# Two common steps, 32 row forms from a table, and loads moved behind a group's first results: attention with routed experts on one core

## The chip, the cores and the metric

The kernel runs on one core of one Trainium2 chip. The time is the device time of one execution in microseconds (us). Engines: PE is TensorE's matmul, PEld its weight load, DVE is VectorE, ACT is ScalarE, POOL is GpSimd, SP is the engine that issues most DMAs.

## What is computed

An attention with a window of local keys and a few global ones (batch 4, 8 heads, 768 positions, 64 per head) gives 3072 rows of 512. Each row goes to one of eight experts:

```python
logits = x @ w_gate
expert_idx = np.argmax(logits, axis=1)
...
gate_w = probs[np.arange(N), expert_idx]
for e in range(E):
    mask = expert_idx == e
    ...
    h = np.maximum(xe @ w1[e], 0.0)
    ye = h @ w2[e]
    out[mask] = gate_w[mask, None] * ye
```

`w1` is 512 x 1024 and `w2` is 1024 x 512 for each expert, all in float32. How many rows an expert gets is known only at run time.

## The kernel before

The first part (to about 160 us) is attention in 24 blocks of 128 rows. Each row is written to a place in HBM that belongs to its expert, and the experts' row counts are made on DVE. The second part takes the experts as *groups* in the order 0, E, 1, 2, ... 7: group 0 is expert 0 without the last sequence's rows, E is the late rest of expert 0 (`plain`, at most 128 rows), and the others are whole experts. This text calls the groups by their expert.

**A group.** Its rows are split in two halves of up to 256 (even and odd rows). `up` (line 993) and `down` (line 1006) multiply with a scheme of seven products of quarter matrices in place of eight (`seven`, line 882). `up` calls it twice (the columns of `w1` in two halves, j = 0 and 1), `down` once: 21 steps. A step of `up` is 4 matmuls of 128 x 128 weights by n rows, a step of `down` 8, where n is the number of rows in a half. DVE and ACT take each product out of PSUM: `one` is copied to p1 by ACT (L904), `two` adds to u2 on DVE (L908), `three` gives c11 through ACT (L913), `four` gives u3 (L919), `five`, `six` and `last` give c22, c21 and c12 (L935, L940, L974). `two` and `four` use the same PSUM bank Y, so `four` can't start before u2 is formed. The operations of DVE and ACT always take all 256 columns, whatever n is.

**Forms.** PE alone has code for several n: `SIZES` (line 675) holds 17 of them, 128 to 256 by 8. `tables` (line 754) works out an index from the group's row count on DVE, with an add, a shift, two copies of types and bounds. `f.hint` reads the index into a register of PE at the group's start, and names the branch target ahead; `emit_forms` (line 271) writes one copy of the group's steps for each size, and a branch with a table of equal strides (L277) goes to the one wanted. Products inside such a copy are cut to n columns (line 259).

**Common steps.** The first steps of a group are not in the forms, so that the branch need not be known at once. With `common` the four steps `one` to `four` of j = 0 are written once for 208 columns (`COMMON`). Forms over 208 make up for the columns past 208 in `rest` (line 921), which is put with `five`. It holds five products, three operations of DVE and two of ACT; DVE and ACT run theirs in every form.

**Order of the work.** The order on each engine is the order in which the code records operations. `group` (line 1329) does this: `run` goes through the steps, and `at_(i, ...)` puts operations behind step i. In a group behind its `one` come two blocks of the previous group's results (`y_out`, j = 1 and 3: four transposes on PE, a gating on ACT, L860, and a scatter on POOL), then `two`, the blocks 0 and 2, `three` and `four`, and then the branch (lines 1360 to 1368). DVE also forms the sums of the weight quarters (`own`, L738 to L741): two behind `one`, one behind `two`.

**Loads.** All are issued by SP in order, and an issue that has to wait holds those behind it. A group's start issues `load_x` for the next group (eight DMAs of rows and two of gate values). Step 10 writes blank rows for the group after next on POOL. Step 14 (`D`) issues the first weights of the group after next, four DMAs of 512 KB, and step 20 (`D + 6`) the second weights, four more (lines 1420 to 1424). There is one buffer for rows and two for weights.

Of the kernel before, what the change touches and what calls it, by code (L numbers as in the profile page):

```python
# [24 lines left out]
class Flow:  # L25
# [214 lines left out]
    def emit(self, op, sems, n, more=0):  # L240
        self.wait(op, sems)
        args, kw = op["args"], op["kw"]
        if op["name"] == "await":
            return
        if op["name"] == "number":
            ap, label = args
            self.loads[label] = self.nc.values_load(
                ap, min_val=0, max_val=1, skip_runtime_bounds_check_because="a comparison's result")
            return
        if op["name"] == "load":  # L250
            index, n, label = args
            self.loads[label] = self.nc.tensor.value_load(index, min_val=0, max_val=n - 1)
            return
        if op["name"] == "hint":
            index, n, label = args
            self.hints[label] = self.loads[label], self.nc.tensor.switch_hint(self.loads[label], n, label)
            return
        if n is not None and op["dyn"]:
            n -= op["past"]
            args = tuple(a[:, 0:n] for a in args[:1]) + tuple(args[1:])  # L260
            kw = dict(kw, rhs=kw["rhs"][:, 0:n])
        call = getattr(self.engines[op["e"]], op["name"])
        where = dict(call=call, args=args, kw=kw)

        exec(_code(*op["at"]), where)
        if op["dma"]:
            where["inst"].then_inc(sems[op["proc"]], 16)
        elif op.get("told") or more:
            where["inst"].then_inc(sems[op["proc"]], int(bool(op.get("told"))) + more)
# [393 lines left out]
class Experts:  # L663
# [8 lines left out]


    P, E, CAP, LATE, COMMON = 128, 8, 512, 128, 208
    SIZES = list(range(128, 257, 8))

    def __init__(self, f, dims, psum, keep, wsets, work, zeros, ylast):
        self.f, self.psum, self.keep = f, psum, keep
# [65 lines left out]
    def slots_table(self):  # L744
        f, k, E = self.f, self.keep, self.E
        for j in range(4):
            f.pool.iota(k["slot4"][:, 0, j:j + 1], pattern=[[0, 1]], base=256 * (j // 2) + j % 2,
                        channel_multiplier=2, allow_small_or_imprecise_dtypes=True)
            f.pool.iota(k["slot4"][:, 1, j:j + 1], pattern=[[0, 1]], base=128 * j,
                        channel_multiplier=1, allow_small_or_imprecise_dtypes=True)  # L750
        f.pool.iota(k["gbase"][:], pattern=[[self.REGION, E + 1]], base=0, channel_multiplier=0,
                    allow_small_or_imprecise_dtypes=True)

    def tables(self, g0, g1, late=False):
        k, V = self.keep, self.f.dve
        n = g1 - g0
        shape = [self.P, n, 4]
        cnt = k["cnt"][:, g0:g1]
        sl = k["slot4"][:, int(late), :].unsqueeze(1).to_broadcast(shape)
        inv = k["inv"][:, g0:g1, :]  # L760
        V.tensor_tensor(inv, cnt.unsqueeze(2).to_broadcast(shape), sl, ALU.is_le)
        V.tensor_scalar(k["inv_i"][:, g0:g1, :], inv, float(2 ** 30), None, ALU.mult)
        V.tensor_scalar(k["is_i"][:, g0:g1, :], inv, 1.0, None, ALU.subtract)
        if late:
            return
        ki, kf = k["ki"][:, g0:g1], k["kf"][:, g0:g1]
        V.tensor_scalar(ki, cnt, 15.0, None, ALU.add)
        V.tensor_scalar(ki, ki, 4, None, ALU.logical_shift_right)
        V.tensor_copy(out=kf, in_=ki)
        V.tensor_scalar(kf, kf, 16.0, 0.0, ALU.subtract, ALU.max)  # L770
        V.tensor_scalar(k["index"][:, g0:g1], kf, 16.0, None, ALU.min)

    def blank(self, g):

# [107 lines left out]
    def seven(self, c, a, s, cols, order, dst, act, half=None, common=False, end=None):  # L882
# [9 lines left out]
        def bank(b):  # L892
            return self.psum[:, b, :].rearrange("p (t c) -> p t c", t=2)

        def mm(b, wq, xq, fresh, half=None, cut=slice(0, 256)):
            self.product(b, [c[wq][:, k, cols] for k in order], [xq[:, k, :] for k in order], fresh, half, cut)
# [18 lines left out]
                f.act.copy(dst["c11"], bank(X))  # L915

        def four():
            mm(Y, "t3", s[2], True, cut=some)
            V.tensor_tensor(u3[:, :, some], u2[:, :, some], bank(Y)[:, :, some], ALU.add)  # L919

        def rest():
            T = self.tbanks[self.tp ^ 1]
            mm(X2, "b11", a["a11"], True, cut=past)
            f.act.copy(p1[:, :, past], bank(X2)[:, :, past])
            mm(Y2, "t2", s[1], True, cut=past)
            V.tensor_tensor(u2[:, :, past], p1[:, :, past], bank(Y2)[:, :, past], ALU.add)
            mm(W2, "b11", a["a11"], True, cut=past)
            mm(W2, "b21", a["a12"], False, cut=past)
            f.act.activation(dst["c11"][:, :, past], bank(W2)[:, :, past], act)
            mm(T, "t3", s[2], True, cut=past)  # L930
            V.tensor_tensor(u3[:, :, past], u2[:, :, past], bank(T)[:, :, past], ALU.add)

        def five():
            mm(W, "t1", s[0], True)
            V.tensor_tensor(dst["c22"], u3, bank(W), ALU.add)  # L935
            relu(dst["c22"])
# [40 lines left out]
        if half:  # L977
            return [one, two, four_end, five_end, six, three, last_end]
        if common:
            return [one, two, three, four, lambda: [rest(), five()], six, last]  # L980
        return [one, two, three, four, five, six, last]

    def h_sums(self, j):
# [55 lines left out]
def kernel(  # L1039
# [46 lines left out]
        ("oh", [P, NBLK, E], BF16), ("slot_i", [P, 2, NBLK], I32), ("ok", [P, 8], F32),  # L1086
        ("flag", [P, 1], I32), ("far", [P, 1], F32), ("slot4", [P, 2, 4], F32), ("gbase", [P, E + 1], F32), ("cnt", [P, E + 1], F32),
        ("inv", [P, E + 1, 4], F32), ("is_i", [P, E + 1, 4], I32), ("padf", [P, E + 1, 4], F32), ("pad", [P, E + 1, 4], I32),
        ("inv_i", [P, E + 1, 4], I32), ("ki", [P, E + 1], I32), ("kf", [P, E + 1], F32),
        ("index", [P, E + 1], I32), ("gt", [P, E + 1, 4, 2], F32), ("to", [P, E + 1, 4], I32))}  # L1090
    ident, iota_p, col, before, ones, rev8, ebase, base_e, tokid = (
        keep[nm] for nm in ("ident", "iota_p", "col", "before", "ones", "rev8", "ebase", "base_e", "tokid"))
# [7 lines left out]
    with ExitStack() as stack:  # L1100
# [225 lines left out]
        for fn in ex.x_sums():  # L1326
            fn()

        def group(p):

            g = order[p]
# [4 lines left out]
            def at_(i, *fns):  # L1336
                todo.setdefault(i, []).extend(fns)
# [8 lines left out]
            if p:  # L1346

                prev = order[p - 1]
                if E not in (g, prev):
                    f.hint(*forms[g])  # L1350
                if nxt is not None and g != E:
                    ex.load_x(nxt, [f"pad{nxt}.{j}" for j in range(4)])
                if nxt is None:
                    f.number(keep["flag"][0:1, 0:1], "redo")
                outs = [0] if prev == E else [1, 3, 0, 2]
                own = ex.w_sums(g, True) + ex.w_sums(g, False) if ups else None
                if ups:
                    at_(0, own[3], own[4])
                    at_(1, own[5])
                    run(ups[:1], 0)  # L1360
                for j in outs[:2]:
                    ex.y_out(prev, j)
                if ups:
                    run(ups[1:2], 1)
                for j in outs[2:]:
                    ex.y_out(prev, j)
                if ups:
                    run(ups[2:4], 2)
            D = 14
            if g != E:  # L1370

# [31 lines left out]
            elif g == E:  # L1403
                sums, pieces, xs = ex.w_sums(1, True), ex.w_pieces(2), ex.x_sums()
                at_(0, sums[0], sums[1])
                at_(1, sums[2], check_sums)
                at_(2, check)
                at_(3, lambda: f.hint(*forms[1]), lambda: ex.x_in(1, 0), lambda: ex.x_in(1, 1), xs[0], xs[1])
                at_(4, xs[2], xs[3], lambda: ex.marks(1), *pieces[:4])
                at_(5, *pieces[4:])  # L1410
            else:
                if nxt is not None:
                    sums, xs = ex.w_sums(nxt, True), ex.x_sums()
                    at_(13, lambda: ex.x_in(nxt, 0))
                    at_(D + 1, lambda: ex.x_in(nxt, 1), sums[0])
                    at_(D + 3, xs[0], xs[1])
                    at_(D + 4, sums[1])
                    at_(D + 5, sums[2])
                    at_(D + 6, xs[2], xs[3], lambda: ex.marks(nxt))
                if after is not None:  # L1420
                    pieces = ex.w_pieces(after)
                    at_(10, lambda: ex.pads(after, ex.h[:, 2:4, 0]))
                    at_(D, *pieces[:4])
                    at_(D + 6, *pieces[4:])

            if g == E:
                ex.plain(0, lambda i: [fn() for fn in todo.pop(i, ())])
                return
            with f.forms(*forms[g]):
                run(ups[4:] if p else ups[2:], 4 if p else 2)  # L1430
                early = ((1, "act"), (3, "dve")) if nxt is None else ()
                run(ex.down(g, (lambda: [ex.y_out(g, j, on) for j, on in early]) if early else None), D)
            assert not todo, todo
# [440 lines left out]
```

## Time and profile before

| | us |
|---|---|
| runs | 500.08, 500.9, 501.0 (median 500.9) |
| profiled execution | 499.16, its span 497.3 |
| granted TensorE clock in it | 0.989 |
| PE busy | 474.0 (95% of the span) |
| DVE busy | 361.4 (73%) |
| all matmuls of the experts (L876) | 288.9 in 1760 rows of the trace |
| PE's last work ends at | 484.3 |

Each float32 matmul is two rows of the trace. Group 2 starts at 255.6 us, group 3 at 292.9, group 4 at 332.7, group 5 at 370.0, group 6 at 411.2 and group 7 at 451.0. The trace has the sequencer's instructions too (moves, branches, hints); the page doesn't count them as busy. A row of idle time names what ended it, as far as the profile can tell.

### The profile page before, as it was taken

How to read it: one execution, taken by the hardware profiler on the slowest of the kernel's cores; microseconds unless marked ns; L12 is line 12 of the kernel's file. 1: busy time of each engine (PE TensorE's matmuls, PEld its weight loads, DVE VectorE, ACT ScalarE, POOL GpSimd, SP SyncE). 2: the span in 40 equal slices, each digit the busy share in tenths (PEclk: the TensorE clock that was granted, in tenths of full speed). 3: DMA queues.
4: the chain of work that ended last, by engine and by line, in shares of the span. 5: the costliest groups of instructions: out<-in, count | busy, mean ns of one | idle time of the engine just before them, and what ended most of it. 6: DMA issues, size and time to landing. Idle time of an engine off the chain costs nothing. (4 is left out here: it accounts for less than half of the span.)

```text
span 497.3 us, 10822 instructions
## 1 busy us (share of the span) xinstructions
PE 474.0 (95%) x4413; PEld 448.9 (90%) x4413; DVE 361.4 (73%) x649; ACT 172.8 (35%) x309; POOL 167.1 (34%) x193
## 2 busy tenths in 40 slices
PE   7899999999998999999999999999999999999990
PEld 6788888887787899999999999999999999999980
DVE  6366779899886884766876886867877676777850
ACT  5665555653654230323123223214214204303410
POOL 2653578567775053302013213204304303003011
PEclk9999999999999999999999999999999999999995
DMA  9999999989524438896864764657567478001000
GB/s 174 204 244 244 198 240 259 235 202 242 149 88 86 171 129 189 207 258 148 189 207 120 186 213 112 155 177 179 128 202 177 111 186 237 3 1 55 14 26 30
DMA packets 120092, 79.24 MB, mean 159 GB/s; under 512 B 86170, under 2 KB 103066, under 8 KB 120020
## 3 DMA queue, kind: packets, MB, share of 16 engines
q1 hardware_dynamic: 112482, 63.52, 55.4%
q0 software_dynamic: 6480, 14.45, 8.1%
q8 instruction: 51, 0.84, 0.7%
q10 hardware_dynamic: 1058, 0.26, 0.3%
q14 instruction: 21, 0.17, 0.1%
HBM read 61.39 MB, written 23.71 MB: 171 GB/s over the span
## 5 line engine op out<-in xcount | busy, mean ns | idle before, releaser
L876 PE MATMUL psum<-arena 128*128 128x208 f32 (+5 forms) x1760 | 288.9, 325 | 0.2
L876 PEld LDWEIGHTS psum<-arena 128*128 128x128 f32 x1760 | 283.6, 190 | 1.8 <-ACT arena L904 0.6
L866 POOL DMA_INDIRECT out_dram<-arena,to x16 | 22.9, 1432 | 170.9 <-ACT arena L860 147.3
L529 DVE TENSOR_TENSOR arena<-psum,arena 128x1024 f32<-128x1024 f32 x40 | 48.3, 1218 | 28.1 <-PE psum L519 28.1
L537 ACT ACTIVATE arena<-arena 128x1024 f32<-128x1024 f32 (+1 forms) x48 | 47.4, 988 | 51.6 <-DVE arena L529 43.8
L543 POOL TENSOR_TENSOR arena<-arena 128x512 f32<-128x512 f32 x40 | 51.9, 1300 | 29.6 <-ACT arena L537 29.3
L900 ACT ACTIVATE arena<-arena 128x512 f32<-128x512 f32 x48 | 30.2, 630 | 53.6 <-DVE arena L935 33.4
L519 PE MATMUL psum<-arena 64*128 64x128 f32 x704 | 46.2, 279 | 1.6 <-ACT arena L505 1.6
L519 PEld LDWEIGHTS psum<-arena 64*128 64x128 f32 x704 | 41.6, 187 | 5.5 <-issue 3.0
L556 PE MATMUL psum<-arena 128*64 128x128 f32 x704 | 43.7, 276 | 0.3 <-issue 0.3
L904 ACT COPY arena<-psum 128x512 f32<-128x512 f32 (+1 forms) x24 | 13.5, 560 | 81.8 <-PE psum L876 81.7
L783 POOL DMA_INDIRECT xg_dram<-small,pad x24 | 23.4, 975 | 51.2 <-ACT arena L913 40.0
L556 PEld LDWEIGHTS psum<-arena 128*64 128x64 f32 x704 | 37.9, 137 | 2.9 <-issue 0.6
L655 POOL DMA_INDIRECT xg_dram<-arena,slot_i x24 | 25.0, 1040 | 21.7 <-DVE arena L974 16.3
L919 DVE TENSOR_TENSOR arena<-arena,psum 128x512 f32<-128x512 f32 (+1 forms) x23 | 15.1, 657 | 22.0 <-PE psum L876 21.9
L974 DVE TENSOR_TENSOR arena<-arena,psum 128x512 f32<-128x512 f32 x23 | 15.8, 687 | 15.9 <-PE psum L876 15.9
L940 DVE TENSOR_TENSOR arena<-arena,psum 128x512 f32<-128x512 f32 x24 | 16.5, 687 | 14.4 <-PE psum L876 14.3
L935 DVE TENSOR_TENSOR arena<-arena,psum 128x512 f32<-128x512 f32 x24 | 16.5, 687 | 14.0 <-PE psum L876 13.9
L866 POOL DMA_INDIRECT out_dram<-ylast,to x17 | 17.0, 999 | 20.4 <-ACT ylast L860 12.5
L908 DVE TENSOR_TENSOR arena<-arena,psum 128x512 f32<-128x512 f32 (+1 forms) x24 | 15.7, 656 | 8.3 <-PE psum L876 7.8
L739 DVE TENSOR_TENSOR arena<-arena 128x1024 f32<-128x1024 f32 x15 | 21.2, 1411 | 0.0
L738 DVE TENSOR_TENSOR arena<-arena 128x1024 f32<-128x1024 f32 x16 | 20.3, 1266 | 1.1 <-DMA arena<-in_moe_w_dram 1.1
(166 smaller groups left out, 552.0 us busy)
## 6 DMA issues: line engine op xcount, KB each, us to landing
arena<-in_moe_w_dram SPq DMA_DIRECT2D x64, 512.0 KB, 6.7
arena<-xg_dram SPq DMA_DIRECT2D x64, 128.0 KB, 6.1
arena<-in_v_dram SPq DMA_DIRECT2D x24, 256.0 KB, 5.6
arena<-in_q_dram SPq DMA_DIRECT2D x23, 256.0 KB, 5.3
arena<-in_k_dram SPq DMA_DIRECT2D x23, 256.0 KB, 5.7
xg_dram<-arena SPq DMA_DIRECT2D x2, 1032.0 KB, 6.2
xg_dram<-arena,slot_i POOLq DMA_INDIRECT x24, 4.5
xg_dram<-small,pad POOLq DMA_INDIRECT x24, 2.1
```

Source lines behind the costliest of these rows:

```text
L519: f.pe.matmul(self.psum[:, 2 * g + a, c:c + P], lhsT=kt[r, m, :], rhs=qt[r, m, :], start=True, stop=True, skip_group_check=True)
L529: f.dve.tensor_tensor(e, s, self.bias[:, g, :, 1:3, :].rearrange("p h k c -> p h (k c)"), ALU.add)
L537: f.act.activation(e, e, AF.Exp)
L543: f.pool.tensor_tensor(self.es[n % 3][:, g], e[:, :, 0:P], e[:, :, P:2 * P], ALU.add)
L556: f.pe.matmul(po[r, m, :], lhsT=self.v[(n - ab) % 6][:, 2 * m + a, :], rhs=self.e[n % 2][:, m // 2, 2 * a + m % 2, P * ab:P * ab + P], sta ...
L655: self.f.pool.indirect_dma_start(out=self.xs[:], out_offset=bass.IndirectOffsetOnAxis(ap=k["slot_i"][:, b % 2, u:u + 1], axis=0), in_=self ...
L738: return [lambda: V.tensor_tensor(c["t3"], c["b22"], c["b12"], ALU.subtract), lambda: V.tensor_tensor(c["t1"], c["b12"], c["b11"], ALU.sub ...
L739: lambda: V.tensor_tensor(c["t1"], c["b12"], c["b11"], ALU.subtract),
L783: self.f.pool.indirect_dma_start(out=self.xs[:], out_offset=bass.IndirectOffsetOnAxis(ap=self.keep["pad"][:, g, j:j + 1], axis=0), in_=sel ...
L866: return pool.indirect_dma_start(out=self.out[:], out_offset=bass.IndirectOffsetOnAxis(ap=self.keep["to"][:, g, j:j + 1], axis=0), in_=sel ...
L876: f.pe.matmul(self.psum[:, bank, 256 * t + cut.start:256 * t + cut.stop], lhsT=w[k][:, ts(t, 128)], rhs=x[k][:, cut], start=(fresh and t = ...
L900: f.act.activation(d, d, act)
```

## The change

Three things are changed. `SIZES` becomes a list of 32 sizes: 128 to 164 by 4, 168 to 206 by 2, 208 and 256. The index is now found by comparing the row count with twice each size and adding up the results; the doubled sizes are written by three iotas of POOL. The common steps are `one` and `two` alone: `three` and `four` go into the forms, `four` is no longer cut at 208 columns, and `rest` loses its part of `four` and stands ahead of it. The row loads of the next group are recorded behind `three` and wait for the first quarter of that step's result. The second weights of the group after next are kept in `owed` and issued in the next group behind these row loads, no longer at step 20.

```diff
         if n is not None and op["dyn"]:
-            n -= op["past"]
+            n = min(n - op["past"], args[0].shape[-1])
...
     P, E, CAP, LATE, COMMON = 128, 8, 512, 128, 208
-    SIZES = list(range(128, 257, 8))
+    RUNS = (range(128, 168, 4), range(168, 208, 2), range(208, 256, 48))
+    SIZES = [n for run in RUNS for n in run] + [256]
...
+        at = 0
+        for run in self.RUNS:
+            f.pool.iota(k["rows"][:, at:at + len(run)], pattern=[[2 * run.step, len(run)]], base=2 * run.start,
+                        channel_multiplier=0, allow_small_or_imprecise_dtypes=True)
+            at += len(run)
...
-        ki, kf = k["ki"][:, g0:g1], k["kf"][:, g0:g1]
-        V.tensor_scalar(ki, cnt, 15.0, None, ALU.add)
-        V.tensor_scalar(ki, ki, 4, None, ALU.logical_shift_right)
-        V.tensor_copy(out=kf, in_=ki)
-        V.tensor_scalar(kf, kf, 16.0, 0.0, ALU.subtract, ALU.max)
-        V.tensor_scalar(k["index"][:, g0:g1], kf, 16.0, None, ALU.min)
+
+        shape = [self.P, n, len(self.SIZES) - 1]
+        over = k["over"][:, g0:g1, :]
+        V.tensor_tensor(over, cnt.unsqueeze(2).to_broadcast(shape), k["rows"][:].unsqueeze(1).to_broadcast(shape),
+                        ALU.is_gt)
+        V.tensor_reduce(k["kf"][:, g0:g1], over, AX.X, ALU.add)
+        V.tensor_copy(out=k["index"][:, g0:g1], in_=k["kf"][:, g0:g1])
...
         def four():
-            mm(Y, "t3", s[2], True, cut=some)
-            V.tensor_tensor(u3[:, :, some], u2[:, :, some], bank(Y)[:, :, some], ALU.add)
+            mm(Y, "t3", s[2], True)
+            V.tensor_tensor(u3, u2, bank(Y), ALU.add)
 
         def rest():
-            T = self.tbanks[self.tp ^ 1]
             mm(X2, "b11", a["a11"], True, cut=past)
...
-            mm(T, "t3", s[2], True, cut=past)
-            V.tensor_tensor(u3[:, :, past], u2[:, :, past], bank(T)[:, :, past], ALU.add)
...
         if common:
-            return [one, two, three, four, lambda: [rest(), five()], six, last]
+            return [one, two, three, lambda: [rest(), four()], five, six, last]
...
+        owed = []
+
         def group(p):
...
                 if nxt is not None and g != E:
-                    ex.load_x(nxt, [f"pad{nxt}.{j}" for j in range(4)])
+
+                    at_(2, lambda: ex.load_x(nxt, [f"pad{nxt}.{j}" for j in range(4)] + [ex.h[:, 0, 0, 0:128]]))
+                at_(2, *owed)
+                owed.clear()
...
-                if ups:
-                    run(ups[2:4], 2)
...
                     at_(D, *pieces[:4])
-                    at_(D + 6, *pieces[4:])
+                    owed.extend(pieces[4:])
...
             with f.forms(*forms[g]):
-                run(ups[4:] if p else ups[2:], 4 if p else 2)
+                run(ups[2:], 2)
```

More of the change, by code (lines that the diff above doesn't have):

```diff
@@ L1088 @@
         ("inv", [P, E + 1, 4], F32), ("is_i", [P, E + 1, 4], I32), ("padf", [P, E + 1, 4], F32), ("pad", [P, E + 1, 4], I32),
-        ("inv_i", [P, E + 1, 4], I32), ("ki", [P, E + 1], I32), ("kf", [P, E + 1], F32),
+        ("inv_i", [P, E + 1, 4], I32), ("kf", [P, E + 1], F32),
+        ("over", [P, E, len(Experts.SIZES) - 1], BF16), ("rows", [P, len(Experts.SIZES) - 1], F32),
         ("index", [P, E + 1], I32), ("gt", [P, E + 1, 4, 2], F32), ("to", [P, E + 1, 4], I32))}
```

## The prediction

> Times below are microseconds after the start of the span, or, with "+", after a group's first pass of `one`. A group is one expert's rows; a pass is one row of the trace on TensorE: a float32 matmul makes two. The chip's own measurement tells about 0.2% (1.0 us) from no change.
>
> **What bounds the kernel now.** First the page's busy rows and its slices, to see which engine fills the routed half. Columns of the first row: busy time, share of the span, instructions.
>
> ```profile
> span 497.3 us, 10822 instructions
> PE 474.0 (95%) x4413; PEld 448.9 (90%) x4413; DVE 361.4 (73%) x649; ACT 172.8 (35%) x309; POOL 167.1 (34%) x193
> ...
> PE   7899999999998999999999999999999999999990
> ```
>
> TensorE is at nine tenths or more from the third slice to the last but one. Then the busy times by stage, cut at the groups' first passes (experts 2, 3, 4, 5, 6, 7 in this order). Columns: stretch, its length, busy time and count on PE, PEld, DVE, ACT and POOL, clock, DMA share, GB/s.
>
> ```profile
> 255.60:292.90 37.30, 37.30 (x242) 37.23 (x241) 29.61 (x41) 9.97 (x18) 9.20 (x8) 1.00 0.65 173
> 292.90:332.70 39.80, 39.80 (x241) 39.73 (x241) 29.62 (x41) 10.08 (x18) 9.20 (x8) 1.00 0.58 158
> 332.70:370.00 37.30, 37.30 (x242) 37.23 (x241) 29.62 (x41) 9.97 (x18) 9.20 (x8) 1.00 0.64 171
> 370.00:411.20 41.20, 41.20 (x243) 41.13 (x242) 29.61 (x41) 10.08 (x18) 9.19 (x8) 1.00 0.63 160
> 411.20:451.00 39.80, 39.80 (x241) 39.73 (x240) 29.61 (x41) 10.08 (x18) 4.41 (x4) 1.00 0.28 76
> 451.00:484.30 33.30, 32.94 (x258) 31.61 (x256) 25.14 (x39) 11.20 (x21) 6.55 (x6) 1.00 0.09 34
> ```
>
> Groups 2 to 6 have no idle TensorE at all, so a pass made shorter there ends the kernel earlier. Group 7, with the fewest rows, has some. Last the row of the branch that enters a form, min/median/max in ns, and VectorE around the entry of group 7 (start, length, operation, idle before it):
>
> ```profile
> L277 PEldq COMPARE_BRANCH  x16: 292/303/938, 165.6 to 483.9; - x16
> ```
>
> ```profile
> 454.01 1.23 DVE L741 TENSOR_TENSOR arena<-arena 128x1024 f32<-128x1024 f32 x1 [0.62 <-issue]
> 455.15 1.22 DVE L738 TENSOR_TENSOR arena<-arena 128x1024 f32<-128x1024 f32 x1
> 456.29 0.58 DVE L908 TENSOR_TENSOR arena<-arena,psum 128x416 f32<-128x416 f32 x1
> ```
>
> L908 forms u2, which frees the bank that `four` writes. It stands behind two weight sums (L741, L738), so it ends at 456.87, +5.84, whatever TensorE does. The branch takes 0.3 us at best but 0.94 at worst: that is the thing to watch.
>
> [...] starts lie 176, 169.2, 155.8, 149 and 116 ns apart at 208, 200, 184, 176 and 136 rows, so 0.835 ns a row; I use that. [...] the trace has such packets of 16,384 bytes on the instruction queue, one between the hint and each branch. [...]
>
> **The change, part by part.**
>
> *Rows.* With the reference's inputs the groups hold 352 (group 0), 416, 361, 397, 367, 410, 395, 271 rows. Half of that, rounded up by 8, gives the forms seen (176, 208, 184, 200, 184, 208, 200, 136). The new table gives 176, 208, 182, 200, 184, 206, 198, 136. A group has 224 passes (each of 14 up products 8, each of 7 down products 16). Before, 32 of them (four steps) are at 208; after, 16. Saved rows times passes: 16 x (208 - new) + 192 x (old - new).
> - group 1: 0; group 2: 416 + 384 = 800; group 3: 128; group 4: 384; group 5: 32 + 384 = 416; group 6: 160 + 384 = 544; group 7: 1152. Group 0 and the late group: 0.
> - Sum 3424 rows x 0.835 ns = 2.86 us, of which group 7 has 0.96.
>
> *Group 7 gives half of it back.* `four` waits for u2 at +5.84. After the change `three` would end at +4.55 + 8 x 0.116 = +5.48, so `four` still starts near +6.0 as before and what `three` saves (0.48) is idle. `four` saves its 0.48; of it some 0.03 goes where `six` waits for u3. I take 0.45 for 0.96. Bounds: 0.2 (VectorE loses more) to 0.96. In groups 2 to 6 u2 ends at +5.27, +5.27, +5.26, +5.26, +5.65 and `four` starts at +4.55 + 8 passes = +5.78 to +5.95: enough, by 0.1 us at the least in group 6.
>
> *The branch moves up.* It now stands behind `two` and the four y blocks, not behind `four`. What the engine waits for last ahead of it was u2 (+5.3 in groups 2 to 5: the moves that begin the branch's sequence start 0.05 to 0.08 after it). It becomes the gate of y block 3 on ScalarE, which ends at +2.69 + 0.68 = +3.37. The sequence is 0.27 us of register work, the branch (0.30) and 0.16 to the next entry: +4.15. TensorE has queued work until +4.55, with the next weight load at +4.45. So 0.25 us are to spare and the cost is nothing, if the code has come. The cover before was `four`, 1.4 us.
>
> *Has the code come?* Its packet starts at +3.49, +3.95, +3.09, +4.04, +2.07, +1.31 in groups 2 to 7 and takes about 1.0. In groups 2, 3 and 5 the branch (467, 858, 938 ns) ended 1.62, 1.47 and 1.48 after the packet did: code is ready about 1.47 after its packet, at +5.9, +6.5, +5.5, +6.5, +4.6 and +3.7. The changed branch wants it by +4.25. Only group 7 has that now, and it is the one with no loads in flight: in the others the last two weight pieces of 512 KB go out at -0.5 and +0.2 and ten row loads from +0.9 to +6, and the DMA share from +1 on is 0.8 to 1.2. The change moves exactly these: rows wait for `three`'s result, about +6.3, and the second weights stand behind them on SP. So the packet should start near group 7's +1.3, code be ready at +3.7. I take no idle time; bounds 0 and 7.8 us (worked out at rival 1).
>
> *The moved loads.* Rows: issued from +6.3 for 4.5 us (eight by 0.55), gate values 1.2, landing some 6 later: about +17; they are read at the end of the up half and its sums, about +22. Second weights: issued from about +12 for some 3 to 6 us, landed by +24; first read at the next group's start, +37. Behind them on SP stand only the first weights of that group, issued at about +18 to +19.5 before and after. POOL's order is not touched but for the table. Cost nothing, with 5 us of cover for the rows; without it the loss would be the lateness itself.
>
> *VectorE, ScalarE, POOL.* u3 is one operation of 0.69 us in place of 0.59 and 0.25. `rest`'s copies (0.24 and 0.26) now stand ahead of u3 on the path to `six`: for 182 rows u3 ends near +8.0 and `six` starts at +8.25. The table: three iotas at 18.6, 0.08 us each from start to start, into 0.26 of idle POOL; on VectorE two short chains of five operations of 0.16 us become three, once in the attention half and once in group 0, while TensorE has work (PE 33.86 of 34.00 in group 0's stretch). Nothing, plus or minus 0.1. Reading 31 columns for 7 experts is not in the trace; at the 0.19 us of the 128x28 compare and 0.69 of 128x512 it is 0.2 to 0.4.
>
> *Sum.* 0.67 + 0.11 + 0.32 + 0.35 + 0.45 + 0.45 = 2.35. The profiled execution took 499.16 (span 497.3 and 1.9 around it), so 496.8 is its counterpart. The runs' median, 500.9, lies 1.7 above it; I keep that distance: 498.55, said as 498.6.
>
> **Rivals.**
> 1. *The branch is late* (slower). If the code's packet isn't sooner than today, the branch ends at +5.9, +6.5, +5.5, +6.5, +4.6 where +4.25 is free: 1.68 + 2.23 + 1.25 + 2.29 + 0.32 = 7.8 us of idle TensorE, less 2.35: 506.3. It is slower as soon as the five groups idle 0.5 us each. For it: these packets were the late ones already. Against: group 7, where an empty queue gave +1.3.
> 2. *The short waits take it* (within 0.2%). Entry takes 0.3 more than I think (a branch of 398 ns as in groups 4 and 6, a weight load that can't run ahead), in six groups 1.5 to 1.8 in all: 500.2. For it: the cover is 0.25 us. Against: the passes behind today's branches show no gap.
> 3. *Group 7 keeps all of its saving*: 2.86 in place of 2.35, 498.0. This is within the forecast's own case.
> 4. *The forms don't shrink.* The table counts sizes under the row count; if it chose 256 rows each time, seven groups would grow by some 65 rows x 208 passes x 0.835 ns = 11 us each: near 580. Nothing in the diff points there.
>
> **How the numbers follow.** Forecast (gain of 1.0 to 3.4): 0.72, time 498.6. Rival 2: 0.13. Rival 1, whole or in part: 0.15. Faster 0.72, same 0.13, slower 0.15. The forecast's own range is 497.4 to 499.9; to hold 8 in 10 it reaches over rival 2 to 501.6, and leaves out most of rival 1.
>
> **What would show it.** Right: passes of 182, 206 and 198 rows; 16 at 208 in each group; groups 2 to 6 at 36.6, 39.7, 37.0, 40.8, 39.4 us, still without idle TensorE; the branch at about 0.3 to 0.4 us; instruction packets near +1.3; group 7 with a gap ahead of `four`. Wrong: a gap between the last y block and `three`, with branches over 0.6 us; u2 or row loads as the releaser of a wait in groups 2 to 6.

## The result and the profile after

| | before | after |
|---|---|---|
| median of 15 runs each, us | 500.66 (499.49 to 502.83) | 498.61 (497.73 to 500.86) |
| ratio, 95% interval | | 0.9966 (0.9954 to 0.9979) |
| profiled execution, its span, us | 499.16, 497.3 | 498.01, 496.1 |
| group 2, 3, 4, 5, 6, 7 from first pass to first pass, us | 37.30, 39.86, 37.30, 41.14, 39.86, 26.60 | 36.63, 39.75, 36.99, 40.79, 39.83, 26.10 |

The changed kernel is faster by 0.34%, some 2 us. The last row comes from the starts of TensorE's passes; group 7 is counted, in every kernel alike, to a point 1.41 us (eight passes of 208 rows) ahead of the first pass of its own results' blocks. First the busy times by stage of the changed kernel, cut at its own first passes.

```profile
256.10:292.70 36.60, 36.60 (x241) 36.53 (x241) 29.50 (x40) 9.86 (x18) 9.21 (x8) 1.00 0.67 177
292.70:332.50 39.80, 39.80 (x243) 39.73 (x242) 29.48 (x40) 9.97 (x18) 9.20 (x8) 1.00 0.62 157
332.50:369.50 37.00, 37.00 (x242) 36.93 (x242) 29.48 (x40) 9.86 (x18) 9.20 (x8) 1.00 0.67 172
369.50:410.30 40.80, 40.80 (x242) 40.73 (x242) 29.48 (x40) 9.98 (x18) 9.18 (x8) 1.00 0.64 161
410.30:450.10 39.80, 39.62 (x241) 39.27 (x240) 29.38 (x40) 10.07 (x18) 4.86 (x4) 1.00 0.35 102
450.10:483.00 32.90, 32.11 (x257) 30.75 (x256) 25.08 (x39) 11.32 (x21) 6.55 (x6) 1.00 0.10 35
```

Groups 2 to 5 are shorter and still without idle TensorE. Group 6 was without idle before and now has some (39.62 busy of 39.80): that is new. The branch row of the changed kernel (min/median/max in ns) shows that the longest branch fell from 938 to 642.

```profile
L277 PEldq COMPARE_BRANCH  x16: 297/310/642, 165.9 to 482.4; - x16
```

It starts at +3.70 in every one of groups 2 to 7. The instruction packets with the forms' code start at +1.08, +1.41, +1.48, +2.00, +1.54 and +1.79; the rows of the next group are issued from +6.7 to +11.5 and the second weights from +11.9 to +13.8, all behind the packet.

Group 6's new idle time lies ahead of `four`. VectorE first, then TensorE (start, length, idle before and its releaser):

```profile
412.47 0.16 DVE L831 TENSOR_TENSOR to<-to,inv_i 128x4 int32<-128x4 int32 x1
413.52 1.22 DVE L742 TENSOR_TENSOR arena<-arena 128x1024 f32<-128x1024 f32 x1 [0.89 <-issue]
414.67 1.22 DVE L739 TENSOR_TENSOR arena<-arena 128x1024 f32<-128x1024 f32 x1
415.80 0.58 DVE L915 TENSOR_TENSOR arena<-arena,psum 128x416 f32<-128x416 f32 x1
```

```profile
416.53 0.91 PE L883 MATMUL psum<-arena 128*128 128x198 f32 x4 [0.18 <-DVE arena L915]
```

VectorE waits 0.89 us for nothing that the profile shows, between the last small operation of group 5 and the first weight sum of group 6. So u2 (L915) ends at 416.38, +6.10, where it ended at +5.65 before, and `four` starts late (around it the starts of the passes lie 0.42 us further apart than their rows ask for). The prediction had named u2 as the releaser of a wait in groups 2 to 6 as a sign of being wrong; here it came, in one group.

A second new wait is in the late group E. The first weight sum of group 1 started at 200.90 before; in the changed kernel, with E's first pass at 198.9 in both, it stands at:

```profile
202.57 1.23 DVE L739 TENSOR_TENSOR arena<-arena 128x1024 f32<-128x1024 f32 x1 [2.76 <-DMA arena<-in_moe_w_dram]
```

```profile
207.24 0.27 PE L1308 MATMUL psum<-ident,ok 128*1 128x128 f32 x1 [0.34 <-DVE ok L1303]
```

The sums hold up a small operation of VectorE (L1303), for whose result a transposition on TensorE waits. By the passes' starts it waits 0.5 us.

### The profile page after: what moved, and what is told of

The parts are those of the page before. It is cut to its first block, busy times and chain, and to the rows that moved or that the text cites. A ratio compares the mean times of both kernels' runs of the same rounds, so it can differ in the third digit from the quotient of the medians.

```text
span 496.1 us, 10821 instructions
## 1 busy us (share of the span) xinstructions
PE 473.4 (95%) x4413; PEld 447.9 (90%) x4413; DVE 355.8 (72%) x638; ACT 172.4 (35%) x309; POOL 166.4 (34%) x196
## 5 line engine op out<-in xcount | busy, mean ns | idle before, releaser
L883 PE MATMUL psum<-arena 128*128 128x208 f32 (+8 forms) x1760 | 286.2, 324 | 0.6 <-DVE arena L915 0.5
L939 DVE TENSOR_TENSOR arena<-arena,psum 128x512 f32<-128x512 f32 x24 | 16.5, 688 | 16.4 <-PE psum L883 13.7
L926 DVE TENSOR_TENSOR arena<-arena,psum 128x512 f32<-128x512 f32 x23 | 15.8, 688 | 17.0 <-PE psum L883 16.2
L978 DVE TENSOR_TENSOR arena<-arena,psum 128x512 f32<-128x512 f32 x23 | 15.8, 688 | 15.4 <-PE psum L883 13.5
L944 DVE TENSOR_TENSOR arena<-arena,psum 128x512 f32<-128x512 f32 x24 | 16.5, 689 | 14.1 <-PE psum L883 12.0
L739 DVE TENSOR_TENSOR arena<-arena 128x1024 f32<-128x1024 f32 x16 | 20.3, 1266 | 2.8 <-DMA arena<-in_moe_w_dram 2.8
L915 DVE TENSOR_TENSOR arena<-arena,psum 128x512 f32<-128x512 f32 (+1 forms) x24 | 15.8, 656 | 8.3 <-PE psum L883 7.9
L742 DVE TENSOR_TENSOR arena<-arena 128x1024 f32<-128x1024 f32 x16 | 19.5, 1221 | 1.7 <-issue 1.5
```

The lines of the kernel that those rows point to most:

```text
L739: return [lambda: V.tensor_tensor(c["t3"], c["b22"], c["b12"], ALU.subtract), lambda: V.tensor_tensor(c["t1"], c["b12"], c["b11"], ALU.sub ...
L742: lambda: V.tensor_tensor(c["t4"], c["b21"], c["t2"], ALU.subtract)]
L883: f.pe.matmul(self.psum[:, bank, 256 * t + cut.start:256 * t + cut.stop], lhsT=w[k][:, ts(t, 128)], rhs=x[k][:, cut], start=(fresh and t = ...
```

## The experiments

Theory: the gain is saved rows times passes; the earlier branch is free only because, with the loads moved, no large load is in flight ahead of the form's instruction packet; where the whole saving isn't seen, u2 or another wait of VectorE is in the way. Rivals: the branch's new place is harmless and the loads don't matter; the table itself slows the entry; the small waits have other causes. The kernels were run in three batches, each with its own runs of the kernel before: 500.95 us for the first four below; 499.71 for rows first, second weights back, four common steps and the sum on POOL; 499.48 for the rest. So ratios are compared, not times. "Idle ahead of `three`" is what the passes' starts show beyond their rows; the packets are those with the code of the form, counted from the group's first pass.

| kernel | packets in groups 2 to 6 | idle ahead of `three`, us | ratio (95%) |
|---|---|---|---|
| changed | 1.1, 1.4, 1.5, 2.0, 1.5 | none | 0.9966 (0.9954 to 0.9979) |
| both loads back | 3.6, 6.0, 3.7, 4.2, 3.6 | 1.85, 4.54, 1.96, 2.11, 1.78 | 1.0286 (1.0250 to 1.0323) |
| rows first | 4.6, 7.6, 4.6, 6.7, 5.6 | 2.63, 5.76, 2.59, 3.25, 2.74 | 1.0415 (1.0384 to 1.0447) |
| second weights back | 3.6, 4.7, 3.6, 4.0, 3.9 | 1.58, 2.60, 1.62, 1.35, 1.96 | 1.0140 (1.0110 to 1.0171) |
| rows alone | 1.5, 4.7, 1.7, 3.6, 4.6 | 0, 3.12, 0, 0.06, 2.52 | 1.0175 (1.0136 to 1.0213) |

In the lower four kernels group 5 also waits inside its `one`, behind the fifth pass, for 0.33, 1.37, 0.53 and 1.58 us. There the packet that belongs to the exit from the form before is late as well: it starts at -1.1 to -0.4, where it starts at -1.7 in the changed kernel, and TensorE goes on 1.3 to 1.55 us after that packet's end.

### Both loads back where they were

```diff
-                    at_(2, lambda: ex.load_x(nxt, [f"pad{nxt}.{j}" for j in range(4)] + [ex.h[:, 0, 0, 0:128]]))
+                ex.load_x(nxt, [f"pad{nxt}.{j}" for j in range(4)])
...
-                    owed.extend(pieces[4:])
+                    at_(D + 6, *pieces[4:])
```

> The changed kernel with row loads and second weights issued where they were before (group start and step 20). Theory (the early branch is free only because the moved loads leave the instruction packet an empty queue): the packets of groups 2 to 5 start near +3.1 to +4.0 again, group 6 near +2, the branch lasts 1.2 to 2.9 us in them, TensorE idles 1.2 to 2.3 us ahead of step three in groups 2 to 5, 7.8 us in all: about 506 us. Rival (the packets came early because of the new layout of the code, not because of the loads): packets stay near +1.5, branches at 0.4 us, time as the changed kernel within 0.3%.

515.38 us. The branch row, and TensorE where group 3 enters its form:

```profile
L277 PEldq COMPARE_BRANCH  x16: 293/308/5259, 166.0 to 497.0; - x16
```

```profile
298.76 1.04 PE L861 MATMUL psum<-ident,arena 128*128 128x128 f32 x8
304.18 2.36 PE L883 MATMUL psum<-arena 128*128 128x200 f32 x6 [4.38 <-issue]
```

Between the last y block and `three` TensorE stands still for 4.4 us, and the branch of 5.26 us ends 1.6 us after its packet. Theory held for the place, and not for the size (some 506 us expected). This is the prediction's first rival, seen whole: with two common steps and the loads in their old place, the kernel loses more than the rows gain.

### The table alone, and the loads alone

Two kernels made from the one before. The first has the 32 sizes and their table:

```diff
-    SIZES = list(range(128, 257, 8))
+    RUNS = (range(128, 168, 4), range(168, 208, 2), range(208, 256, 48))
+    SIZES = [n for run in RUNS for n in run] + [256]
```

> The kernel before with the 32 sizes alone; four common steps and loads as before. Theory (a pass costs 0.835 ns a row, nothing else changes): 192 passes by 2 rows less in groups 2, 5 and 6, 1152 rows, so 0.96 us less than before, group spans 36.98, 40.82 and 39.54 us. Rival (twice as many copies make the entry slower: branch and packets): the branches of groups 2 to 6 lengthen by more than 0.5 us over before's and the gain is under 0.3 us.

507.56 us, ratio 1.0134 (1.0102 to 1.0165). Groups 2 and 5 got 0.32 us shorter as their rows ask for, but in group 6 the form's packet doesn't start until +10.21:

```profile
L277 PEldq COMPARE_BRANCH  x16: 292/305/6229, 166.7 to 491.9; - x16
```

```profile
416.34 3.04 PE L882 MATMUL psum<-arena 128*128 128x208 f32 x16
424.66 1.66 PE L882 MATMUL psum<-arena 128*128 128x198 f32 x4 [5.29 <-issue]
```

Neither side came as written: the kernel isn't faster, but only the branches of groups 4 and 6 grew by over 0.5 us, and group 4's is covered. The loss is group 6's.

The second has the loads moved and the old sizes:

```diff
-                    ex.load_x(nxt, [f"pad{nxt}.{j}" for j in range(4)])
+                    at_(2, lambda: ex.load_x(nxt, [f"pad{nxt}.{j}" for j in range(4)] + [ex.h[:, 0, 0, 0:128]]))
+                at_(2, *owed)
+                owed.clear()
...
-                    at_(D + 6, *pieces[4:])
+                    owed.extend(pieces[4:])
```

> The kernel before with only the loads moved behind step three. Theory: packets start near +1.5 in groups 2 to 6 in place of +2 to +4, the branch lasts about 0.3 to 0.4 us in all, and the time stays within 0.2% of before, since branch and rows were covered. Rival (the loads collided with something else too): faster than before by over 0.5 us; or slower, with row loads as the releaser of a wait.

500.9 us, ratio 1.0003 (0.9986 to 1.0021). Packets come at +1.3, +1.9, +1.6, +2.5, +0.9, no branch takes longer than 402 ns:

```profile
L277 PEldq COMPARE_BRANCH  x16: 288/300/402, 166.3 to 485.5; - x16
```

The group spans are those of before. Theory held. With four common steps the branch lies behind `four`, where before the change too it cost nothing, so an earlier packet brings nothing by itself.

### u2 ahead of the second sum

```diff
-                    at_(0, own[3], own[4])
-                    at_(1, own[5])
+                    at_(0, own[3])
+                    at_(1, own[4], own[5])
```

> The changed kernel with VectorE's second weight sum recorded behind step two's u2 in place of ahead of it. Theory (u2 is late behind two weight sums, which idles TensorE 0.42 us ahead of step four in group 6 and 0.54 in group 7): u2 ends 1.14 us sooner, at +4.1 in groups 2 to 5 and +5.0 and +4.7 in groups 6 and 7, both gaps close, and about 0.9 us goes. Rival (VectorE is simply full at that place, so the sum that is moved makes u3 late in its stead): the gaps move to six or last, gain under 0.3 us.

499.3 us, ratio 0.9962 (0.9948 to 0.9976). u2 ends 0.7 to 1.1 us sooner (+4.97 in group 6, +4.71 in group 7). Group 6 takes 39.40 us: its gap is closed, so u2 was what `four` waited for. That is the theory's half. Group 7 stays at 26.14, since the idle time moves to `six` (0.8 us), which waits for u3 behind the sum recorded later: the rival's half. The whole can't be told apart from the changed kernel; E's wait was 0.9 us in the profiled execution.

### One load back at a time

The row loads put back to the group's start, the second weights left in `owed`:

```diff
-                    at_(2, lambda: ex.load_x(nxt, [f"pad{nxt}.{j}" for j in range(4)] + [ex.h[:, 0, 0, 0:128]]))
+                ex.load_x(nxt, [f"pad{nxt}.{j}" for j in range(4)])
```

> The changed kernel with only the row loads put back to the group's start; the second weights stay behind three. Theory: [...] both loads count by the bytes that move between the hint and the packet. The rows (1 MB in eight DMAs, issued from +0.9 to +6) overlap that stretch more than the two last weight pieces do: packets at +2.5 to +3.5, branches of 1.2 to 2.4 us, 0.8 to 1.8 us idle ahead of three in each of groups 2 to 6, and 503 to 507 us in all. Rival A (the weights alone do it): packets stay under +2, branches under 0.65, 498.5 to 499.5 us. Rival B (the rows alone do it): the time of both put back, 512 us or more.

521.03 us. The number lies in rival B's range, but not for its reason: it is more than with both back. SP's issues show why:

```profile
289.80 3.76 SPq L814 DMA_DIRECT2D arena<-xg_dram  x8
293.61 1.18 SPq L823 DMA_DIRECT2D gt<-xg_dram  x2
294.83 2.93 SPq L722 DMA_DIRECT2D arena<-in_moe_w_dram  x4
```

Group 3 starts at 295.28. The second weights were recorded behind `three`, but they wait only for their own buffer; what held them in the changed kernel is the row loads' wait for `three`. Without it SP runs ahead and issues both loads around the hint (at -1.2). So this kernel isn't the rows alone. Its expectation took a later place in the program for a later time.

The second weights put back to step 20, the rows left behind `three`:

```diff
-                    owed.extend(pieces[4:])
+                    at_(D + 6, *pieces[4:])
```

> The changed kernel with only the second weights put back to step 20 of the group before; the rows stay behind three. Theory (both loads count, the rows more): packets at +2 to +3, branches of 0.6 to 1.8 us, 0.2 to 1.2 us idle ahead of three in groups 2 to 5 (the later groups have no weights left to load), 500 to 503 us. Rival A (the weights alone do it): 512 us or more, as with both put back. Rival B (the rows alone do it): packets under +2, branches under 0.65, 498.5 to 499.5 us.

507.26 us, over the range of the theory, under that of rival A. Of the two loads only the weights are in flight here (the rows are issued from +8.4 on), and every packet of groups 2 to 6 is later than in the changed kernel, by 2.0 to 3.3 us:

```profile
L277 PEldq COMPARE_BRANCH  x16: 297/312/3312, 165.6 to 491.6; - x16
```

```profile
259.34 1.04 PE L861 MATMUL psum<-ident,arena 128*128 128x128 f32 x8
261.80 1.49 PE L883 MATMUL psum<-arena 128*128 128x182 f32 x8 [1.42 <-issue]
```

To have the rows alone, the second weights got a wait of their own for `three`'s first quarter (each of the four DMAs names it as read), with the rows at the group's start as above:

```diff
-            out.append(lambda d=w["w2"][:, c:c + 2, :], s=s[:, c:c + 2, :]: f.sp.dma_start(out=d, in_=s))
+            out.append(lambda d=w["w2"][:, c:c + 2, :], s=s[:, c:c + 2, :]:
+                       f.sp.dma_start(out=d, in_=s, _r=list(held)))
...
-                    pieces = ex.w_pieces(after)
+                    pieces = ex.w_pieces(after, [ex.h[:, 0, 0, 0:128]])
```

> The changed kernel with the rows issued at the group's start as SP comes to them (from about -5.5 to -1.7, since nothing stands ahead), and the second weights held by a wait for three's first result, so that they are not in flight when the code is fetched. In the run where only the order of the rows was put back, both loads ran early. Theory (the code waits for the bytes in flight between the hint at -1.6 and its packet; the 1 MB of rows takes some 6 us to land, to about +4 for the last): packets at +2 to +3.5, 0.3 to 1.8 us idle ahead of three in each of groups 2 to 6, 500 to 506 us. Rival (only the weights, which come last, hold the packet up): packets under +2, no idle, 498.0 to 499.5 us.

509.6 us. It is neither case throughout. In groups 2 and 4 the last of the row loads is issued at -5.8 and -4.5 and the packets come at +1.5 and +1.7; in groups 3 and 5 the last goes out at -1.7 and the packets start at +4.7 and +3.6. But in group 6 it goes out at -4.6, as in group 4, and the packet starts at +4.6 all the same; see below. After group 3's gap the clock column (behind POOL's) tells of a second cost:

```profile
297.20:300.20 3.00, 0.06 (x1) 0.00 (x0) 1.73 (x3) 0.98 (x2) 2.39 (x3) 0.89 0.27 93
300.20:304.00 3.80, 3.79 (x11) 3.79 (x12) 0.00 (x0) 0.57 (x2) 1.83 (x2) 0.50 0.36 130
304.00:308.00 4.00, 4.00 (x18) 4.00 (x18) 1.27 (x3) 0.34 (x2) 0.00 (x0) 0.70 0.73 217
```

Group 3 took 46.0 us, 6.25 more than in the changed kernel, of which the gap is half. So the weights do harm by themselves, in every group from 2 to 6 (1.35 to 2.60 us idle with the rows held back). That the rows do is likely from groups 3 and 5, but not shown, since group 6 is late without them.

### Four common steps with the table and the moved loads

```diff
-            return [one, two, three, lambda: [rest(), four()], five, six, last]
+            return [one, two, three, four, lambda: [rest(), five()], six, last]
...
+                if ups:
+                    run(ups[2:4], 2)
```

(`four` and `rest` are as before the change, too.)

> The 32 sizes and the moved loads, but four common steps as before the change: what the two shorter common steps bring is the difference to the changed kernel. Theory: only groups 2, 5 and 6 change against before, by 2 rows x 192 passes x 0.835 ns = 0.32 us each (36.98, 40.82 and 39.54 us), branches under 0.65 us everywhere, and the gap of some 0.5 us in the late group that every kernel with the 32 sizes has shown: 500.95 - 0.96 + 0.5 = 500.5 us (499.9 to 501.0). So the common steps bring some 1.9 us, the table nothing. Rival (32 forms make the entry slow whatever the loads do): branches of 1 to 6 us as in the run with the table alone, 502 us or more.

503.01 us, ratio 1.0063 (1.0042 to 1.0084), with runs from 500.28 to 505.31. Groups 2 to 5 took what was expected (36.98, 39.86, 37.30, 40.82), but in group 6 the packet starts at +6.98, 0.6 us after the branch itself, and TensorE waits 2.2 us. The profiled run is the fastest, of 500.28 us; where the others lost up to 5 us more was not traced:

```profile
L277 PEldq COMPARE_BRANCH  x16: 292/306/2969, 165.1 to 484.9; - x16
```

```profile
419.81 1.41 PE L882 MATMUL psum<-arena 128*128 128x198 f32 x7 [2.03 <-issue]
```

So the rival's time came, but in the profile by one group, not at every entry. The run with the table alone and the one with the rows alone had the same: in group 6 no packet between the exit's (-2.1 to -1.5) and the time after the branch has started. What became of that hint is not shown, nor why it was so in these kernels and not in the changed one.

### The old sizes with two common steps

```diff
-    RUNS = (range(128, 168, 4), range(168, 208, 2), range(208, 256, 48))
-    SIZES = [n for run in RUNS for n in run] + [256]
+    SIZES = list(range(128, 257, 8))
```

The index is worked out as before the change.

> Two common steps and the moved loads with the 17 old sizes: what the table adds is the difference to the changed kernel. Theory: 16 passes a group get (208 - n) rows shorter with n of the old sizes: groups 2 to 7 take 36.98, 39.75, 36.98, 41.14, 39.75 to 39.95 (VectorE's branch is at its 696th instruction, wait 0.8 us, so up to 0.2 ahead of four) and 26.1 us, no gap in the late group (it came with the 32 sizes alone), code's packets at +1 to +2: 1.25 us less than before, ratio 0.9975 (0.997 to 0.998). Rival 1 (the gap in the late group comes with the moved code, not with the table): 0.5 more, 0.9985. Rival 2 (with the old sizes a code packet comes late somewhere, as with the 32 sizes and four common steps): a group with 2 us of idle, 501 us or more.

498.46 us, ratio 0.9971 (0.9958 to 0.9985). Groups 2 to 7: 36.98, 39.75, 37.03, 41.17, 39.97, 26.10, and no wait in the late group. Theory held. Most of the change's gain comes from the two shorter common steps with the moved loads; by the profiles the table takes another 0.35 to 0.4 us each in groups 2 and 5 and 0.14 in group 6, and pays for it with 0.5 in E. The two ratios can't be told apart.

### The sum on POOL

```diff
-                    at_(0, own[3], own[4])
+                    c = ex.quarters(g, True)
+                    at_(0, lambda: f.pool.tensor_tensor(c["t4"], c["b21"], c["t2"], ALU.subtract), own[4])
```

> The changed kernel with the first of the two weight sums behind one (t4 of the first weights) made by POOL in place of VectorE. Theory (the gap ahead of four in groups 6 and 7 is u2 queued behind two sums of 1.2 us): u2 ends 0.7 to 1.2 us sooner, no gap ahead of four or six in groups 6 and 7, which take 39.4 and 25.6 us, in all 0.9 us less than the changed kernel, 497.7 us (497.2 to 498.2). Rival 1: POOL's sum takes over 3 us or slows VectorE's beside it (its sums over 1.3 us), and six waits for it in every group: 499 us or more. Rival 2: the gaps move to six as in the run that recorded one sum later: group 7 stays at 26.1 and the time at 498.2 to 498.6.

504.94 us, ratio 1.0101 (1.0069 to 1.0133). POOL and VectorE around the start of group 3:

```profile
292.88 2.35 POOL L1369 TENSOR_TENSOR arena<-arena 128x1024 f32<-128x1024 f32 x1 [15.37 <-DVE arena L741]
```

```profile
294.04 1.75 DVE L849 TENSOR_TENSOR arena<-arena 128x512 f32<-128x512 f32 x1
295.71 0.68 DVE L850 TENSOR_TENSOR arena<-arena 128x512 f32<-128x512 f32 x1
```

POOL's sum takes 2.35 us, to 295.23, and an operation of VectorE that starts beside it (L849) takes 1.75 in place of 0.68. It ends 0.56 us after POOL's; so it is in all of groups 2 to 7 (0.54 to 0.56). What holds it up is not shown, and not every operation beside a sum is held up: L978, from 293.44 to 294.13, took its usual 0.69. u2 ends hardly sooner (+6.05 in group 6). In E, L1303 took 1.82 in place of 0.16 and TensorE waited 2.0 us. Of rival 1 the slower VectorE came, but `six` waited nowhere in groups 2 to 7. The end of the kernel got 4.9 us longer by a wait of POOL ahead of its last two stores (3.47 in the changed kernel):

```profile
491.40 0.97 POOL L873 DMA_INDIRECT out_dram<-ylast,to  x1 [8.37 <-remote]
```

Seven instructions more are on POOL in this kernel, and instruction packets stand in the trace at 489.4 to 489.8. That the wait is for code is argued, not shown. This wait and E's are most of the 6.7 us by which the kernel is slower than the changed one.

### VectorE's code shifted, and three repairs

Sixteen small copies, four in each of groups 1 to 4:

```diff
+                    if 2 <= p <= 5:
+                        at_(D + 2, *4 * [lambda: f.dve.tensor_copy(out=keep["ok"][:, 7:8], in_=keep["far"])])
```

> The changed kernel with sixteen more small copies on VectorE (128x1, 0.16 us), four in the down half of each of groups 1 to 4, where VectorE has idle time; they change nothing that is read. Theory (VectorE's wait behind its branch at the start of group 6 depends on where in its code that branch stands: 585 ns at its 701st traced instruction, 800 at the 697th, 1036 at the 692nd, so some 50 ns an instruction): at the 708th it is 190 to 300 ns, u2 of group 6 ends near +5.3 in place of +6.1, no gap ahead of four, group 6 takes 39.40 us in place of 39.83, and the time is 0.4 us under the changed kernel's, 0.9957 of before. Rival (the wait belongs to what group 6 waits for, data or a signal): it stays at 1.0 us and group 6 at 39.8.

497.29 us, ratio 0.9957 (0.9941 to 0.9974). VectorE at the start of group 6:

```profile
410.99 0.16 DVE L831 TENSOR_TENSOR to<-to,inv_i 128x4 int32<-128x4 int32 x1
411.19 1.23 DVE L742 TENSOR_TENSOR arena<-arena 128x1024 f32<-128x1024 f32 x1
```

The wait of 0.89 us is gone, u2 ends at +5.26, and there is no gap ahead of `four`: the wait came with the place of VectorE's code, as expected. Group 6 took 39.62, not 39.40, since its branch was 0.83 us long this time (packet at +1.97) and `three` 0.2 late. The gain over the changed kernel, 0.0009, lies within the intervals.

The same copies, the flag's load (0.54 us on VectorE ahead of group 7's sums) moved to group 1, and group 1's first weights issued ahead of E's rows:

```diff
-                if nxt is None:
+                if p == 2:
                     f.number(keep["flag"][0:1, 0:1], "redo")
...
-                    ex.load_x(E, last)
                     for fn in pieces[:4]:
                         fn()
+                    ex.load_x(E, last)
```

> The changed kernel with three repairs: the sixteen small copies on VectorE as in the run with them alone; the load of the flag into every engine's registers at group 1's start in place of group 7's; the first weights of group 1 issued ahead of the late group's rows in place of behind them. Theory: the late group's idle of 0.5 us goes (the weight sums start 1 to 2 us sooner), group 6 takes 39.40 us, and u2 of group 7 ends 0.6 us sooner (+5.25), so that group 7 takes 25.6 to 25.8 us in place of 26.1: 1.2 to 1.4 us less than the changed kernel, 0.9940 of before (0.993 to 0.995). Rival 1 (the weights ahead make the late group's rows late): 0.5 to 2 us of idle at the end of group 0. Rival 2 (in group 7 the wait moves from four to six, as when a sum was recorded later): group 7 stays at 26.1.

498.23 us, ratio 0.9981 (0.9966 to 0.9997). By place each did what it should: group 6 at 39.40, group 7 at 25.62, no wait in E. But E's rows came late: in group 0 VectorE stood still for their gate values, and TensorE behind it:

```profile
196.61 0.16 DVE L830 TENSOR_TENSOR to<-gt,is_i 128x1 int32<-128x1 int32 x1 [4.53 <-DMA gt<-xg_dram]
```

```profile
197.62 1.16 PE L883 MATMUL psum<-arena 128*128 128x176 f32 x6 [1.48 <-DVE arena L939]
```

That is rival 1. No version is shown to beat the changed kernel; the shift and the earlier flag load without the third repair were not tried together.

## Why the prediction was right, point by point

- **Rows.** Passes of 182, 206 and 198 rows, groups 2 to 5 at 36.63, 39.75, 36.99, 40.79 for 36.6, 39.7, 37.0, 40.8: right, term by term.
- **Group 7 gives half back.** It saved 0.50 for 0.45 taken of 0.96; u2 at +5.84, 0.54 us idle ahead of `four`. Right.
- **The branch moves up.** It starts at +3.70 and ends at +4.1 to +4.3, and the passes' starts show no idle time behind it. Cost nothing: right, and the 0.25 us to spare were enough.
- **Has the code come?** Predicted near +1.3, measured +1.08 to +2.00. The reason given, the loads, is what the runs with loads put back show; by which path they hold the packet up is not shown. Its other bound, 7.8 us, was too low: with both loads back the idle time is 12.2 us in groups 2 to 6, since group 3's packet came later than before, and slow clock is added (0.59 granted over the 3.8 us behind group 3's gap).
- **The moved loads.** No wait for rows or second weights in groups 2 to 6; the kernel with the loads alone has the ratio 1.0003. Right. What was not said: that the second weights are held only by the rows' wait.
- **Group 6, wrong by 0.4 us.** The step failed at "0.1 us at the least in group 6": u2's end was carried over from before, where at +5.65 it already stood 0.4 us late. The cause of that lateness hadn't been asked for. It is the wait at VectorE's own branch at the start of the group, which grew from 585 to 1036 ns as nine instructions less stood ahead of it.
- **VectorE and POOL, "nothing, plus or minus 0.1": wrong by 0.5 us.** E's wait was not in it. In the profiles of the kernels with 17 sizes (before, the loads alone, two common steps) the sums start 1.5 to 2.0 us after E's first pass; in those with 32 sizes, but for the one with weights issued earlier, 2.9 to 4.1, and TensorE waits in all but the one at 2.9 (the shifted code). In the latter the third scatter in group 0 takes 1.45 us in place of 1.22, and group 1's weights are issued 0.5 to 1.0 us later than before the change. So the wait comes with the table; by which path is not shown.
- **The sum.** 2.35 was predicted from groups 2 to 7; they gave 1.97. Less E's 0.5 it is 1.5, and the profiled span fell by 1.2. The medians differ by 2.05. So 498.61 against 498.6 is closer than the working deserves, and luck: the profiled execution came 1.2 us over its forecast, but lies 0.6 under its median, where 1.7 was assumed from before.
- **Rivals.** The late branch is real: with both loads back the ratio is 1.0286 in place of 0.9966, some 16 us; the change's own third part prevents it. The short waits did come (0.9 us in two places), not at the entry.

## What to carry to other kernels

The branch into a form cost nothing here when nothing large was in flight between the hint and its packet (packets at +1.1 to +2.0, no idle TensorE; group 6 of three kernels, with 2.2 to 5.3 us idle, stays unexplained); with the second weights in flight it idled TensorE for 1.35 to 5.76 us a group, unless queued work covered it. So count what the queues move then, and hold loads back by a wait on data, since a later place in the program held nothing (second weights recorded behind `three` went out at -0.45 in group 3). When work is taken off the critical engine, ask of every wait that had only 0.1 us to spare what sets its length. A part can be worth nothing by itself (the loads alone, 1.0003) and still be what another part needs: the shorter common steps gain with it (0.9971) and lose without it (1.0286, with the table).

## What the runs showed of the hardware

- **VectorE's wait at a branch goes with its place in the code.** At the start of group 6: 1036 ns at its 692nd instruction in the trace (the changed kernel), 846 at the 696th (two common steps, old sizes), 800 at the 697th (the table with four common steps), 585 at the 701st (before), 190 at the 708th (the shifted code), about 50 ns an instruction. In all six kernels in which it is the 692nd the wait is the same within 2 ns, though the loads differ. What in the place makes the wait is not shown.
- **Slow clock after a gap.** After idle times of 2.5 to 5.8 us TensorE's clock fell to half in some groups (passes of 200 rows at 333 ns in place of 169), for 3.41 us three times and for 6.83 us three times, but not after gaps of 2.6, 2.7 and 3.25 us in others. With the rows alone, group 3's gap of 3.12 us was followed by 3.8 us at a granted clock of 0.50 and 4.0 us at 0.70.
- **A branch that waited ended some 1.3 to 1.7 us after its instruction packet did**, in all runs in which one waited: 1.47 to 1.62 before the change (groups 2, 3 and 5), 1.35 in groups 5 and 7 of the changed kernel (packets to 372.45 and 453.10, branches to 373.80 and 454.44), 1.6 in group 3 with both loads back.
